# One queue for every load and store, row copies for the gathers, and 64-column value products in a windowed-attention kernel with token routing

## The chip, the cores and the metric

The kernel runs on one core of a Trainium2 chip. Its time is the device time of one execution in microseconds (us), the median over runs. All other times come from one profiled execution of the kernel before, counted from the start of its span. TensorE is called PE, VectorE DVE, ScalarE ACT, GpSimd POOL and SyncE SP, as in the profile.

## What is computed

Attention with a sliding window of 128 positions and 4 sink tokens, over 4 batches, 8 heads, 768 positions and 64 columns a head; then, in each batch, the 128 tokens with the highest gate score go through a two-layer network and are added back.

```python
scores = scale * np.matmul(q, k.transpose(0, 1, 3, 2))
keep = is_sink | in_window
scores = np.where(keep, scores, -1000000000.0)
a = softmax(scores)                       # cut: max, exp, sum
attn = np.matmul(a, v)                    # [4, 8, 768, 64] -> x [4, 768, 512]
...
scores = np.einsum('bsd,d->bs', x, w_gate)
for b in range(B):
    top_idx = np.argpartition(-scores[b], capacity)[:capacity]    # capacity = 128
    xe = x[b, top_idx]
    ye = np.maximum(xe @ w1, 0.0) @ w2                            # 512 -> 1024 -> 512
    g = 1.0 / (1.0 + np.exp(-scores[b, top_idx]))
    out[b, top_idx] = x[b, top_idx] + g[:, None] * ye
```

## The kernel before

**Steps.** The main loop has 30 steps. Batch 0 takes 12 half steps (steps 0 to 5 for four of its heads, then 6 to 11 for the other four, six blocks j of 128 positions each); batches 1, 2 and 3 take six full steps each (12 to 17, 18 to 23, 24 to 29; all eight heads). The order of all work is written out by hand: functions are hung on a step with `before` (ahead of the step), `middle`, `at` (after its normalisation) and `late`, and each engine executes its instructions in exactly that order.

**One step.** `scores` for step i+2 (PE, into PSUM, then an exponential on ACT, L251); `values` of step i (PE): sink products (L272) and products of the probabilities with the values, 65 columns wide, since a column of ones gives the softmax sum; `norm` (DVE): reciprocal (L300) and two multiplications (L303) into the row tile x; `gate_score` (DVE, L307): the gate's dot product. `values` has one pair of PSUM banks, X, so the products of step i+1 start when `norm` of step i has read it. `store` (L512) sends x of step i-1 to the output from SP's queue.

**Value products.** The stationary operand is a piece of the probabilities, float32, 128 or 64 rows by 64 query columns; each product becomes two PE instructions. Most are 64 columns wide (L262), and two or four of them stand in different parts of the array. For heads 4 to 7 the middle block is one product with 128 columns (L285), except at j = 1, where the key of the sink products makes two 64-column products of it (L281 to L284).

**Loads.** A "head pair" (k and q of two heads, 384 KB each) is loaded by `load_pair` (L126), cast to bf16 by `cast_pair` (mostly POOL, L141), transposed on PE (L172), and copied out of PSUM by DVE (L177) or ACT (L179). Batch 0's pairs come through SP's and ACT's queues at the start; all others through POOL's queue, batch 1's at step 2, batch b+1's right behind the casts of batch b (L585 to L589). Values are loaded in chunks of 128 positions (`load_v`, L143) through SP's queue: batch 1's seven chunks all ahead of step 0, batch 2's one a step from step 8, batch 3's from step 14 (L521 to L524). The weights w1 and w2 are loaded by POOL at step 22, and the first waits for chunk 3 of batch 3 (L528 to L534).

**Ranks.** For batches 0 and 1 the gate scores go to memory (`bounce_out`, L310, into srow) and back as one row broadcast to all partitions (`bounce_in`, L313, into sbc); both DMAs are issued by ACT, in the middle of steps 12 and 13 (18 and 19 for batch 1). `rank_c` (DVE, L317) counts the larger scores, `select` (L348) makes a selection matrix, `chosen` (L353) turns it into row numbers idx. Batches 2 and 3 rank on the chip (`spread`, `compare`, `overtake`).

**Gather and scatter.** `gather` (L380, POOL, indirect DMA) reads the chosen rows from the output tensor for batches 0 to 2, where the row number counts from the tensor's start, and from the row copy xrow for batch 3, which `store` also writes. The network is `ffn_cast` (POOL, L390), `ffn_in`, `ffn_1`, `ffn_2`, `ffn_out`; the last scatters the rows into the output with another indirect DMA (L417). Regions of the output and the row copies are tracked: a gather over rows [0, 2x768) of the output and a scatter into rows [0, 768) are ordered by a wait.

**Semaphores.** The program gives the DMAs of SP and ACT eight completion semaphores in rotation, in the order in which the program is written, whichever of the two issues them; a DMA is issued once the one that held its semaphore before has landed.

Of the kernel before, what the change touches and what calls it, by code (L numbers as in the profile page):

```python
# [8 lines left out]
FP32 = mybir.dt.float32  # L9
# [6 lines left out]
B = 4  # L16
# [17 lines left out]
def kernel(  # L34
# [46 lines left out]
    rankl = [one([128, NB], FP32, "rankl"), x0[:, NB - 2, 16:16 + NB]]  # L81
# [27 lines left out]
    xrow = tc.dram_tile([S, DM], FP32, name="xrow")  # L109
    idl = x0[:, NB - 2, 0:1].bitcast(U32)  # L110
# [15 lines left out]
    def load_pair(b, hp, eng=pool):  # L126
        hs = slice(2 * hp, 2 * hp + 2)
        for t, src in enumerate((k, q)):
            eng.dma_start(out=raw[2 * hp + t][:, :, :, :].rearrange("p h c d -> p h (c d)"),
                          in_=src[b, hs, :, :].rearrange("h (p c) d -> p h (c d)", c=NB))  # L130
# [122 lines left out]
    def values(b, j, heads, bank, which):  # L253
# [26 lines left out]
        for hh in heads:  # L280
            if j == 1:  # L281
                mm(1, 0, hh, FULL, j, 1, j)
                mm(1, 1, hh, FULL, j, 2, j)
                continue  # L284
            pe.matmul(out=ps[:, bank + 1, hh * SK:hh * SK + SK], lhsT=p[j][:, HP + hh, 64:192],  # L285
                      rhs=s.v[1][:, hh, j, 0:SK], start=(1, 0) not in seen, stop=False, skip_group_check=True)
            seen.update(((1, 0), (1, 1)))
# [22 lines left out]
    def bounce_out(b):  # L310
        act.dma_start(out=srow[b, :].rearrange("(p c) -> p c", c=NB), in_=st[b].scol[:, :])

    def bounce_in(b):  # L313
        act.dma_start(out=sbc[:, :], in_=srow[b, :].partition_broadcast(128))
# [38 lines left out]
    def chosen(b, bank, e=E):  # L353
# [6 lines left out]
        if b == B - 1:  # L360
            chl = x0[:, NB - 2, 8:9]
            dve.tensor_scalar_add(out=chl[:, :], in0=ch[:, 1:2], scalar1=-float((B - 1) * S))
        dve.tensor_scalar(out=idx[b][:, :], in0=ch[:, 0:1], scalar1=128.0, scalar2=ch[:, 1:2],
                          op0=ALU.mult, op1=ALU.add)
        if b == B - 1:
            dve.tensor_scalar(out=idl[:, :], in0=ch[:, 0:1], scalar1=128.0, scalar2=chl[:, 0:1],
                              op0=ALU.mult, op1=ALU.add)
# [12 lines left out]
    def gather(b):  # L380
        if b == B - 1:
            src, ix, n = xrow, idl, S
        else:
            src, ix, n = flat, idx[b], (b + 1) * S
        pool.indirect_dma_start(out=xe[b % 3][:, :], out_offset=None, in_=src[0:n, :],
                                in_offset=bass.IndirectOffsetOnAxis(ap=ix[:, 0:1], axis=0),
                                bounds_check=n - 1, oob_is_err=False)
# [33 lines left out]
    with tc.manual_schedule():  # L421
# [3 lines left out]
        load_pair(0, 0, sp)  # L425
        load_pair(0, 2, act)
        load_v_first(0)
        load_pair(0, 1, sp)
        load_pair(0, 3, sp)
# [78 lines left out]
        def store(i):  # L508
# [4 lines left out]
            if b == B - 1:  # L513
                sp.dma_start(out=xrow[j * 128:(j + 1) * 128, :], in_=xt[(b, j)])
# [6 lines left out]
        for c in range(NB + 1):  # L521
            before(0, lambda c=c: load_values(1, c))
            before(8 + c, lambda c=c: load_values(2, c))
            before(14 + c, lambda c=c: load_values(3, c))  # L524
# [3 lines left out]
        def load_weights():  # L528
            for n in range(2):
                i = pool.dma_start(out=w1_sb[:, 2 * n:2 * n + 2, :], in_=w1r[:, 2 * n:2 * n + 2, :])  # L530
                if n == 0:
                    after(i, arrived[(B - 1, 3)])
# [20 lines left out]
        for b, i, js in ((0, 12, (14, 15, 16, 16, 17, 18)), (1, 18, (20, 21, 22, 23, 24, 25))):  # L553
# [24 lines left out]
        for hp in range(HP):  # L578
            before(2, lambda hp=hp: load_pair(1, hp))
# [5 lines left out]
        for b, i0 in ((1, 6), (2, 12), (3, 18)):  # L585
            for hp in range(HP):
                before(i0 + hp - 2, lambda b=b, hp=hp: cast_pair(b, hp))
                if b < B - 1:
                    before(i0 + hp - 2, lambda b=b, hp=hp: load_pair(b + 1, hp))  # L589
# [32 lines left out]
        for i, (b, j, g) in enumerate(steps):  # L622
# [26 lines left out]
            if i == 5:  # L649
                pool.iota(iota_i[:, :], pattern=[[1, 128]], base=0, channel_multiplier=0)  # L650
                pool.iota(tk_i[:, 0:B, :], pattern=[[NB, B], [1, NB]], base=0, channel_multiplier=0)
# [71 lines left out]
```

The softmax here doesn't subtract the row's maximum and nothing guards it: scores larger than these inputs give would overflow.

## Time and profile before

| | |
|---|---|
| time, median of 3 runs (lowest to highest) | 162.63 us (162.05 to 163.7) |
| span of the profiled execution | 161.5 us |
| PE busy | 133.3 us (82%), 2595 instructions |
| PE weight loads busy | 103.5 us (64%) |
| DVE busy | 91.9 us (57%) |
| ACT busy | 78.5 us (49%) |
| POOL busy | 75.6 us (47%) |
| moved by DMA | 32.41 MB, 201 GB/s over the span |
| value products with 128 columns, L285 | 160 instructions, 24.2 us, 291 ns each |
| value products with 64 columns, L262 | 1120 instructions, 38.6 us, 232 ns each |
| head pairs from POOL's queue | 24 DMAs of 384 KB, 7.4 and 7.6 us from issue to landing |

Busy time is the union of the time in which an engine executes; matmuls overlap, so the mean length of one is far above the distance from one to the next, and only the timeline shows the latter. Instructions that issue DMAs don't count as busy. An engine's idle time is put down to what ended it; where a wait has several causes, to the one that came last. A busy share over the whole span hides that stretches have different bounds, so stretches are looked at one by one.

### The profile page before, as it was taken

The numbers are of one execution on the slowest core, as the hardware profiler recorded it, in microseconds if no ns is written. First come the engines' busy times: TensorE is split into PE (matmuls) and PEld (weight loads), VectorE is DVE, ScalarE is ACT, GpSimd is POOL, SyncE is SP. The second block draws the span as 40 slices with busy tenths as digits, with TensorE's granted clock in tenths as the row PEclk, the third lists the DMA queues.
The fourth block names the chain that finished last, engine by engine and source line by source line (L and its number), as shares of the span: only waits on it lengthen the run. The fifth ranks groups of instructions, "written<-read, shape, count | busy, mean of one in ns | idle before, by whom it ended". The sixth has DMA issues, their size and how long they took to land. (4 is left out here: it accounts for less than half of the span.)

```text
span 161.5 us, 6069 instructions
## 1 busy us (share of the span) xinstructions
PE 133.3 (82%) x2595; PEld 103.5 (64%) x2599; DVE 91.9 (57%) x283; ACT 78.5 (49%) x106; POOL 75.6 (47%) x123
## 2 busy tenths in 40 slices
PE   6697989998999029979999997999899599986820
PEld 2255767786788016777788886788776389765500
DVE  6831351568447300664989687779957817376310
ACT  3269266577770043965657578566355102131300
POOL 8637999996997500219106148301202544040520
PEclk9999999999999965999999999999999956999985
DMA  4999899999799998942474343999616333040311
GB/s 111 364 232 343 195 234 381 394 371 365 211 361 339 366 359 238 245 137 86 130 203 140 109 134 80 202 203 235 224 50 199 127 133 127 7 189 10 96 46 55
DMA packets 37658, 32.41 MB, mean 201 GB/s; under 512 B 26992, under 2 KB 30448, under 8 KB 37632
## 3 DMA queue, kind: packets, MB, share of 16 engines
q1 hardware_dynamic: 31456, 16.78, 36.6%
q0 software_dynamic: 5056, 13.67, 27.4%
q10 hardware_dynamic: 1120, 1.58, 3.5%
q8 instruction: 20, 0.33, 0.8%
q14 instruction: 6, 0.05, 0.1%
HBM read 25.20 MB, written 8.92 MB: 211 GB/s over the span
## 5 line engine op out<-in xcount | busy, mean ns | idle before, releaser
L251 ACT ACTIVATE pt<-ps 128x1024 f32<-128x1024 f32 x48 | 47.2, 1034 | 5.8 <-PE ps L229 4.6
L262 PE MATMUL ps<-vbuf,pt 64*64 64x65 f32 (+1 forms) x1120 | 38.6, 232 | 0.7 <-DVE x L303 0.7
L262 PEld LDWEIGHTS ps<-vbuf,pt 64*64 64x64 f32 (+1 forms) x1120 | 30.5, 140 | 11.8 <-issue 8.3
L300 DVE RECIPROCAL rz<-ps 128x8 f32<-128x8 f32 (+1 forms) x30 | 5.9, 196 | 50.5 <-PE ps L262 50.5
L186 POOL COPY ksk<-KT 64x4 bf16<-64x4 bf16 x32 | 9.1, 284 | 33.2 <-ACT KT L179 15.1
L285 PE MATMUL ps<-vbuf,pt 128*128 128x65 f32 x160 | 24.2, 291 | 0.0
L141 POOL CAST kq<-raw 128x768 bf16<-128x768 f32 x28 | 23.1, 852 | 1.7 <-DMA raw<-in_k_dram 0.8
L179 ACT COPY QT<-ps 128x768 bf16<-128x768 bf16 x16 | 12.9, 803 | 19.0 <-DMA out_dram<-x 11.1
L285 PEld LDWEIGHTS ps<-vbuf,pt 128*128 128x128 f32 x160 | 20.7, 199 | 1.8
L172 PE MATMUL ps<-ident_b,kq 128*128 128x128 bf16 x192 | 14.4, 225 | 8.5 <-ACT QT L179 7.1
L213 PE MATMUL ps<-QT,KT 64*64 64x192 bf16 (+2 forms) x384 | 17.4, 248 | 4.6 <-ACT QT L179 2.6
L303 DVE TENSOR_TENSOR x<-ps,rz 128x256 f32<-128x256 f32 (+1 forms) x60 | 19.5, 366 | 1.2
L307 DVE CUSTOM_DVE_ANT_0 junk<-x,wgb 128x512 f32<-128x512 f32 x24 | 19.0, 794 | 0.4
L172 PEld LDWEIGHTS <-kq 128*128 128x128 bf16 x192 | 11.6, 100 | 10.8 <-issue 7.2
L213 PEld LDWEIGHTS <-KT 64*64 64x64 bf16 x384 | 10.5, 107 | 9.8 <-issue 5.9
L272 PE MATMUL ps<-vsk,psk 64*64 64x260 f32 (+1 forms) x180 | 15.6, 358 | 0.9 <-DVE x L303 0.9
L229 PE MATMUL ps<-mask,ident_b 64*64 64x256 bf16 (+1 forms) x208 | 15.3, 264 | 0.0
L317 DVE TENSOR_SCALAR_CACHE_REDUCE junk<-sbc,scol 128x768 bf16<-128x768 f32 x12 | 12.2, 1012 | 0.4
L646 POOL CAST x<-x 128x512 bf16<-128x512 f32 x6 | 4.2, 706 | 15.5 <-DVE x L303 8.8
L323 ACT COPY sbl<-ps 128x128 f32<-128x128 f32 x12 | 3.1, 260 | 15.7 <-PE ps L321 15.7
L417 POOL DMA_INDIRECT out_dram<-y,idx x4 | 4.1, 1023 | 13.8 <-DVE y L415 10.1
L177 DVE COPY KT<-ps 128x768 bf16<-128x768 bf16 x10 | 9.5, 951 | 1.5 <-PE ps L172 1.5
(94 smaller groups left out, 170.9 us busy)
## 6 DMA issues: line engine op xcount, KB each, us to landing
out_dram<-x SPq DMA_DIRECT2D x24, 256.0 KB, 3.7
raw<-in_k_dram POOLq DMA_DIRECT2D x12, 384.0 KB, 7.4
raw<-in_q_dram POOLq DMA_DIRECT2D x12, 384.0 KB, 7.6
vbuf<-in_v_dram SPq DMA_DIRECT2D x33, 128.0 KB, 5.3
w_sb<-in_moe_w_dram POOLq DMA_DIRECT2D x4, 512.0 KB, 9.8
xrow<-x SPq DMA_DIRECT2D x6, 256.0 KB, 3.9
raw<-in_k_dram SPq DMA_DIRECT2D x3, 384.0 KB, 4.0
raw<-in_q_dram SPq DMA_DIRECT2D x3, 384.0 KB, 5.0
```

What stands on the lines that cost most here:

```text
L141: (eng or pool).tensor_copy(out=o, in_=i)
L172: pe.transpose(out=trp[:, c, :], in_=src[:, c, :, :].rearrange("p h d -> p (h d)"), identity=ident_b[:, :])
L179: act.copy(out=o, in_=i)
L213: pe.matmul(out=sc[64 * m:64 * m + 64, e, a, o:o + n], lhsT=s.KT[r, hp, k0:k0 + 64], rhs=s.QT[r, hp, k0:k0 + n], start=a == 0, stop=False, ...
L229: pe.matmul(out=o, lhsT=ident_b[r, r], rhs=w[r].unsqueeze(1).to_broadcast((64, a.stop - a.start, 2, 64)), start=False, stop=True, skip_gro ...
L251: act.activation(out=po[:, gi, :, :, :], in_=sc[:, :, :, :], func=ACT.Exp, scale=0.125)
L262: pe.matmul(out=ps[64 * c:64 * c + 64, bank + be, hh * SK:hh * SK + SK], lhsT=p[i][rows, h, 64 * slot:64 * slot + 64], rhs=s.v[be][rows, h ...
L272: pe.matmul(out=ps[64 * c:64 * c + 64, bank + be, a * SK:z * SK], lhsT=s.psk[which][r, c, 64 * (j - 1):64 * j], rhs=vsk[r, b, be, a:z, :], ...
L285: pe.matmul(out=ps[:, bank + 1, hh * SK:hh * SK + SK], lhsT=p[j][:, HP + hh, 64:192], rhs=s.v[1][:, hh, j, 0:SK], start=(1, 0) not in seen ...
L303: dve.tensor_tensor(out=xo[:, e, :, :], in0=xg[:, e, :, 0:D], in1=rz[:, e, 0:n, :].to_broadcast((128, n, D)), op=ALU.mult)
L307: dve.tensor_tensor_reduce(out=junk[:, :], in0=x, in1=wgb[:, :], scale=1.0, scalar=0.0, op0=ALU.mult, op1=ALU.add, accum_out=st[b].scol[:, ...
L317: dve.tensor_scalar(out=junk[:, :].bitcast(BF16)[:, 0:S], in0=sbc[:, :], scalar1=st[b].scol[:, c:c + 1], scalar2=0.0, op0=ALU.is_gt, op1=A ...
```

## The change

It has four parts.

1. **One queue.** `load_pair` uses SP by default (batch 0's pair 2 stays on ACT); so do `bounce_out` and `bounce_in`. After the start, ACT issues no DMA, and POOL only the weights, the gathers and the scatters.
2. **Order of need.** Pairs of batch 1 are loaded one a step at steps 0 to 3, batch 2's at 6, 8, 9 and 11, batch 3's at 13 to 16. Values of batch 1 come one chunk a step from step 4, batch 2's from step 12, batch 3's from step 16. The weights wait for chunk 5 of batch 3. Batch 0's ranks move by a step here and there (step 14 no longer has one).
3. **Row copies.** Batches 1, 2 and 3 each get a row copy; `store` writes every row tile of these twice, and `gather` reads from the copy with row numbers counted from the batch's start. Only batch 0's gather reads the output. `chosen` makes two row numbers, for the gather (idl) and for the scatter (idx).
4. **64-column products.** `values` uses two 64-column products for the middle block of heads 4 to 7 at every j.

It is meant to keep transfers from colliding, to free ACT and POOL from issuing them, to take the order between gathers and scatters away, and to use the form of product that keeps parts of the array working side by side.

```diff
-    def load_pair(b, hp, eng=pool):
+    def load_pair(b, hp, eng=sp):
...
         for hh in heads:
-            if j == 1:
-                mm(1, 0, hh, FULL, j, 1, j)
-                mm(1, 1, hh, FULL, j, 2, j)
-                continue
-            pe.matmul(out=ps[:, bank + 1, hh * SK:hh * SK + SK], lhsT=p[j][:, HP + hh, 64:192],
-                      rhs=s.v[1][:, hh, j, 0:SK], start=(1, 0) not in seen, stop=False, skip_group_check=True)
-            seen.update(((1, 0), (1, 1)))
+            mm(1, 0, hh, FULL, j, 1, j)
+            mm(1, 1, hh, FULL, j, 2, j)
...
     def bounce_out(b):
-        act.dma_start(out=srow[b, :].rearrange("(p c) -> p c", c=NB), in_=st[b].scol[:, :])
+        sp.dma_start(out=srow[b, :].rearrange("(p c) -> p c", c=NB), in_=st[b].scol[:, :])
     def bounce_in(b):
-        act.dma_start(out=sbc[:, :], in_=srow[b, :].partition_broadcast(128))
+        sp.dma_start(out=sbc[:, :], in_=srow[b, :].partition_broadcast(128))
...
-        dve.tensor_scalar(out=idx[b][:, :], in0=ch[:, 0:1], scalar1=128.0, scalar2=ch[:, 1:2],
+        dve.tensor_scalar(out=(idl[b] if b else idx[0])[:, :], in0=ch[:, 0:1], scalar1=128.0, scalar2=ch[:, 1:2],
                           op0=ALU.mult, op1=ALU.add)
-        if b == B - 1:
-            dve.tensor_scalar(out=idl[:, :], in0=ch[:, 0:1], scalar1=128.0, scalar2=chl[:, 0:1],
+        if b:
+            chl = x0[:, NB - 2, 32:33]
+            dve.tensor_scalar_add(out=chl[:, :], in0=ch[:, 1:2], scalar1=float(b * S))
+            dve.tensor_scalar(out=idx[b][:, :], in0=ch[:, 0:1], scalar1=128.0, scalar2=chl[:, 0:1],
                               op0=ALU.mult, op1=ALU.add)
...
     def gather(b):
-        if b == B - 1:
-            src, ix, n = xrow, idl, S
-        else:
-            src, ix, n = flat, idx[b], (b + 1) * S
-        pool.indirect_dma_start(out=xe[b % 3][:, :], out_offset=None, in_=src[0:n, :],
+        src, ix = (xrow[b], idl[b]) if b else (flat, idx[0])
+        pool.indirect_dma_start(out=xe[b % 3][:, :], out_offset=None, in_=src[0:S, :],
...
             sp.dma_start(out=out[b, j * 128:(j + 1) * 128, :], in_=xt[(b, j)])
-            if b == B - 1:
-                sp.dma_start(out=xrow[j * 128:(j + 1) * 128, :], in_=xt[(b, j)])
+            if b:
+                sp.dma_start(out=xrow[b][j * 128:(j + 1) * 128, :], in_=xt[(b, j)])
...
-            before(0, lambda c=c: load_values(1, c))
-            before(8 + c, lambda c=c: load_values(2, c))
-            before(14 + c, lambda c=c: load_values(3, c))
+            before(4 + c, lambda c=c: load_values(1, c))
+            before(12 + c, lambda c=c: load_values(2, c))
+            before(16 + c, lambda c=c: load_values(3, c))
...
-                    after(i, arrived[(B - 1, 3)])
+                    after(i, arrived[(B - 1, 5)])
...
-        for b, i, js in ((0, 12, (14, 15, 16, 16, 17, 18)), (1, 18, (20, 21, 22, 23, 24, 25))):
+        for b, i, js in ((0, 12, (15, 15, 16, 17, 17, 18)), (1, 18, (20, 21, 22, 23, 24, 25))):
...
-        for hp in range(HP):
-            before(2, lambda hp=hp: load_pair(1, hp))
+        for b, at_ in ((1, (0, 1, 2, 3)), (2, (6, 8, 9, 11)), (3, (13, 14, 15, 16))):
+            for hp, i in enumerate(at_):
+                before(i, lambda b=b, hp=hp: load_pair(b, hp))
...
                 before(i0 + hp - 2, lambda b=b, hp=hp: cast_pair(b, hp))
-                if b < B - 1:
-                    before(i0 + hp - 2, lambda b=b, hp=hp: load_pair(b + 1, hp))
```

## The prediction

> **What bounds the kernel now.** I read the map of the span in 40 slices first, to see where TensorE (PE) is busy and where its clock is low.
>
> ```profile
> PE   6697989998999029979999997999899599986820
> DVE  6831351568447300664989687779957817376310
> ACT  3269266577770043965657578566355102131300
> PEclk9999999999999965999999999999999956999985
> DMA  4999899999799998942474343999616333040311
> ```
>
> PE is 80 to 100% busy in nearly all slices between 8 and 145 us, so its instruction stream sets the pace. Three exceptions: a hole in slices 13 and 14, counted from 0 (52 to 60 us), a halved clock behind it, and a second halved clock in slices 32 and 33 (129 to 137 us). The DMA row is at 9 until 64 us and low afterwards.
>
> The timeline around the hole says who made it:
>
> ```profile
> 51.12 2.21 SPq L512 DMA_DIRECT2D out_dram<-x  x1
> ...
> 58.38 0.35 ACTq L311 DMA_DIRECT2D srow<-scol  x1
> 58.77 0.80 ACT L179 COPY QT<-ps 128x768 bf16<-128x768 bf16 x1 [11.14 <-DMA out_dram<-x]
> ...
> 59.62 0.69 PE L172 MATMUL ps<-ident_b,kq 128*128 128x128 bf16 x5 [7.12 <-ACT QT L179]
> ```
>
> ScalarE (ACT) does nothing for 11.14 us: the small DMA of L311 stands in its instruction stream, and the program gives hardware DMAs eight completion semaphores in rotation, so L311 must wait for the DMA eight before it, a store in SyncE's (SP's) backlogged queue. PE waits behind ACT for 7.12 us. The table by stretch gives the size:
>
> ```profile
> 52.50:59.60 7.10, 0.00 (x0) 0.00 (x0) 1.34 (x4) 0.83 (x2) 2.06 (x3) 0.86 1.09 368
> 59.60:66.00 6.40, 6.09 (x96) 4.62 (x96) 0.00 (x0) 3.83 (x5) 0.36 (x2) 0.62 0.92 241
> ...
> 126.00:128.50 2.50, 0.59 (x7) 0.31 (x3) 2.40 (x9) 0.36 (x2) 2.25 (x3) 1.00 0.26 100
> 128.50:137.00 8.50, 8.47 (x104) 7.38 (x104) 4.20 (x15) 1.45 (x3) 3.29 (x4) 0.60 0.43 153
> ```
>
> Columns: length, busy time of PE, weight loads, VectorE (DVE), ACT, POOL, then granted clock, DMA share, GB/s. No matmul in the first stretch, clock 0.62 and 0.60 in the stretches behind both gaps.
>
> Last, the timeline of two whole steps, j=1 of batch 2 and j=2 of batch 2:
>
> ```profile
> 84.88 1.78 PE L262 MATMUL ps<-vbuf,pt 128*64 128x65 f32 x64
> ...
> 86.58 0.49 PE L321 MATMUL ps<-ident_f,scol 128*128 128x128 f32 x2
> ...
> 88.78 0.69 PE L262 MATMUL ps<-vbuf,pt 128*64 128x65 f32 x16
> ...
> 89.40 1.11 PE L285 MATMUL ps<-vbuf,pt 128*128 128x65 f32 x8
> ...
> 90.43 0.69 PE L262 MATMUL ps<-vbuf,pt 64*64 64x65 f32 x32
> ...
> 91.06 0.30 PE L356 MATMUL ps<-tok,E 128*128 128x4 bf16 x6
> ```
>
> This is the measurement of the new form inside the old kernel. Step j=1 already uses 64-column products only: 64 matmuls from 84.88 to the next work at 86.58, 1.70 us. Step j=2 computes the same with 128-column products: 16 + 8 + 32 matmuls from 88.78 to 91.06, 2.28 us. Its eight 128-column ones take 89.40 to 90.43, 129 ns each; the 64-column ones before them 39 ns each (0.62 over 16).
>
> **What the Trainium skill says.** "TensorEngine Tiling (Array Packing)", Key Properties: a change of tiling mode drains the array, and different tiles run in parallel. The trace agrees on the second: 39 ns against 129 ns with twice as many instructions; a drain is not shown apart. "TensorE: Matmul & The Clock Gate", What's actually happening: the clock halves after an idle window of about 3.4 us and returns after a busy one. The 7.1 us hole agrees. The second dip follows a stretch in which PE worked 0.59 of 2.5 us, shorter than that window, so here a nearly idle window was enough. "DMA: Bandwidth & Descriptors", Issuing engines are not separate DMA queues: moving transfers between engines saves issue time only, all share 16 engines. The trace agrees in that the share stands near 1.0 up to 64 us, whichever queues feed it.
>
> **The change, part by part.**
>
> *64-column products.* Per full step (batches 1 to 3, not j=1): 2.28 - 1.70 = 0.58 us of PE. Per half step of batch 0: 1.36 us with 128 columns (17.86 to 19.22) against 0.85 and 1.01 for the two j=1 half steps, so 0.35 to 0.51, taken as 0.43. Batch 0 has 10 such half steps, each on the path since the next products wait for DVE's normalisation of these: 4.3 us. For full steps I check DVE, which needs its own time per step. Between normalisations it is busy without idle in steps 18, 23 and 24 (3.55 of 3.69 us in 106.28:109.97, 4.25 of 4.39 in 109.97:114.36): those give nothing, step 18 the 0.3 us that DVE waited. Left are steps 12, 14 to 17, 20 to 22 and 26 to 29: 12 x 0.58 + 0.3 = 7.3 us. Between both bounds (all 15: 8.7; half: 4) I take 7.3.
>
> *ACT's small DMAs go to SP.* The hole goes: 7.1 us. The slow stretch 59.6 to 66.0 (transposes, scores, products) takes 6.4 us and at full clock about 4.5 (0.4 for the rest of the transposes, 1.2 for scores, 2.9 for sink and other products, as at 72.8 to 75.7): 1.9 us. Sum 9.0. ACT's later bounce (81 to 87 us) costs PE nothing now.
>
> *Loads just in time, pairs from POOL to SP.* POOL loses 24 issues of 0.72 us, 17.4 us; its casts are ahead of need (PE waits for POOL 0.7 us in all), so worth nothing by itself. The question is whether SP keeps up. In order of SP's queue I add up the bytes (pair 0.79 MB, a chunk of values 0.26, a store 0.26): start 5.0 MB, all of batch 1's pairs 8.1, step 6 9.6, step 12 14.6, step 13 16.6, step 17 22.4. Rates of the trace: 315 GB/s between 12.9 and 46.1 us, 382 in its best quarter. At 350 these are there at 16, 25, 29, 44, 49 and 66 us. PE would want batch 1's last pair at about 34 us, batch 2's first at 43, step 13's rank row at 55, step 17's loads only 3 or more steps later than 63. So hidden, but with little slack for the two rank rows (sbc, 4.2 us to landing, behind srow, 4.1): DVE's rank instructions would stand in front of a normalisation. Bounds 0 and 8 us; I take 1 us for each row, 2.0.
>
> *Row copies.* 12 more stores (3.1 MB, 0.4 us of SP each); from 80 us on the DMA row is mostly at 3 or 4, so the later ones hide. Gather 1 no longer conflicts with scatter 0, which POOL held from 123.3 to 126.2 us (idle 3.4 before L417), nor gather 2 with its landing. The cast for FFN 1 thus comes earlier than 127.84, and PE's wait for it (0.7, weight loads 0.9) goes: 0.8 us. PE's other wait there, 1.2 us for the copy of the chosen tokens (L321 on DVE ch), stays, as its order on DVE does. So I leave the second clock dip in the forecast. DVE gains two small operations in two selections, 0.15 + 0.21 us each, beside PE work.
>
> *Tail.* From the last products (139.9) to the end the chain of selection and FFN is unchanged: 0.
>
> Sum: 162.6 - 4.3 - 7.3 - 9.0 - 0.8 + 2.0 = 143.2 us.
>
> **Rivals.**
> 1. *The second clock dip goes too, and SP keeps up.* The gap at 126 us shrinks from 2.4 to about 1.9 us. Work of 128.5 to 137 at full clock: products 2.3 instead of 3.9, FFN 1.95 instead of 2.9, sink products and spread 0.5 less, so 3.0 us, and 2.0 of waits fewer: 138.2. For it: the gap was a near miss by the skill's window; against: the 1.2 us wait stays.
> 2. *DMA takes over.* Everything is in one queue in order, each DMA waits for the eighth before it, and steps 13 to 16 each want 1.5 MB in 3.4 us, 440 GB/s, over any rate in the trace. At 305 GB/s (36.5 to 46.1) the 23 MB up to step 18 end at 77 us, where PE would be at about 64; with 5 us of order slack in the stores' four buffers, 8 us more: 151. For it: the full DMA row up to 64 us. Against: what is late by then is needed latest.
> 3. *Slower.* SP stands at a bounce (srow landing before sbc) while loads queue behind it; DVE stands at ranks, PE goes cold each time. To lose, new waits must exceed 21 us: three holes like the old one, 7.1 + 1.9 each, give 143.2 - 2.0 + 27 = 168. For it: the old hole had just this form, one DMA behind another's landing. Against: it now stands in SP, where nothing computes.
>
> **How the numbers follow.** Forecast 0.52, rival 1 0.25, rival 2 0.17, rival 3 0.06. The range runs from 137 (rival 1 with all 15 steps gained) to 152 (rival 2) and leaves out rival 3 and some edges. Faster by over 1%: 0.93, within 1%: 0.02, slower: 0.05.
>
> **What would show it.** Right: no L285-like 128*128 product group, the products of a full step in 1.7 us; no ACT wait on a DMA; PE over 80% busy at 45 to 60 us; clock 1.0 there. Wrong: DVE idle before a rank (L312 in the new file) on sbc, normalisation or casts waiting on a store or load, PE idle behind them; or steps that keep their length with DVE full, which would mean that the products were not the bound.

## The result, and the profile after

The changed kernel takes 152.33 us (median of 4 runs, 149.12 to 154.33), the kernel before 162.34 us beside it. The ratio, 0.922 with a 95% interval of 0.909 to 0.936, leaves out executions that are over 1.5% above the fastest of their kernel, as the ratios below do, so here it is that of 149.12 and 150.53 us; the medians of all would give 0.938. The forecast of 143.2 us was too low by 9 us against the median, which lies 0.3 us above the upper end of its range, 137 to 152, and by 6.6 us against the mean of those two, which lie inside it. Executions of one kernel differ here by 3 us and more, so below a total is given as a median with its lowest and highest, and what a part is worth is read from the traces. Each trace is one execution; where it is a long one of its kernel, the text says so.

The profiled execution of the changed kernel took 150.53 us, its span is 148.8 us. Its map in 40 slices (3.7 us each):

```profile
PE   6687989998989987669799920998989969977940
DVE  6851172569438464098988306778996696688520
ACT  3169467598887875365746780055827232323310
PEclk9999999999999999999999997589999999999995
DMA  3999969987999999999999799899995346332031
```

The hole at 52 to 60 us and the low clock behind it are gone, and so is the low clock near the end (slices 32 and 33). A new hole stands in slices 23 and 24 (86 to 93 us): PE at 2 and 0, DVE at 0 in the first of them, then a clock of 0.5 to 0.8. The DMA row is at 6 to 9 until slice 29 (112 us), where it used to fall at 64 us.

The table by stretch (length, busy time of PE, weight loads, DVE, ACT, POOL, then clock, DMA share, GB/s), the first three where the old hole and its surroundings were:

```profile
42.80:49.80 7.00, 7.00 (x192) 5.93 (x188) 4.78 (x14) 5.06 (x7) 2.49 (x3) 1.00 1.08 355
52.50:59.60 7.10, 5.55 (x160) 4.32 (x157) 3.88 (x10) 4.82 (x6) 3.76 (x9) 1.00 0.98 275
59.60:66.00 6.40, 3.85 (x104) 2.82 (x100) 2.92 (x7) 3.43 (x5) 2.18 (x4) 1.00 1.11 355
82.30:92.90 10.60, 4.35 (x126) 3.46 (x117) 2.90 (x11) 5.83 (x8) 2.36 (x5) 0.90 0.95 273
92.90:98.00 5.10, 5.07 (x76) 3.91 (x78) 3.34 (x12) 0.02 (x1) 3.62 (x5) 0.54 0.88 212
123.00:129.90 6.90, 6.90 (x181) 5.69 (x179) 4.27 (x15) 2.30 (x6) 3.17 (x4) 1.00 0.53 186
```

PE works where it stood before, but only 5.55 of 7.1 us and 3.85 of 6.4 us. The fourth and fifth line are the new hole and its cold clock.

The timeline says what the new hole waits for. Step 17 is the last block of batch 1; its gate score is read at 70.46 us:

```profile
70.46 0.08 DVE L302 DVE_READ_ACCUMULATOR2_ANT scol<- 128x1 f32 x1
...
80.22 0.41 SPq L306 DMA_DIRECT2D srow<-scol  x1
...
82.92 1.78 PE L262 MATMUL ps<-vbuf,pt 128*64 128x65 f32 x64
83.97 0.32 SPq L309 DMA_DIRECT2D sbc<-srow  x1
...
90.70 1.01 DVE L312 TENSOR_SCALAR_CACHE_REDUCE junk<-sbc,scol 128x768 bf16<-128x768 f32 x1 [7.63 <-DMA sbc<-srow]
...
92.93 1.46 PE L272 MATMUL ps<-vsk,psk 64*64 64x260 f32 x8 [5.47 <-DVE x L298]
```

SP issues the small DMA of the row 9.8 us after the score is there. DVE then stands 7.63 us at the first rank instruction (L312), behind it the normalisation of step 21 (L298), behind that PE. SP hardly idled in these 9.8 us: fourteen issues of loads and stores lie between, 0.4 to 1.2 us each, 8.5 us together; why one takes three times as long as another is open. None of them waited for a landing: wherever it is recorded (thirteen of the fourteen), the DMA eight places earlier had landed before SP was free. In the table of waits:

```profile
DVE junk L312 <- DMA sbc<-srow: 11.9, 2, 7.6
...
PE ps L272 <- DVE x L298: 8.6, 5, 5.5
```

(Columns: total us, number, longest.) The products of a full step now take 1.78 us for 64 matmuls (the line at 82.92), as in step j=1 before.

For what follows I cut each trace at the start of DVE's reciprocal of certain steps. "End" is the end of the span. The forecast's column puts its terms into the same stretches: 0.43 us for each half step and 0.58 for each full step it counted (a step's products lie ahead of its own reciprocal), 9.0 for the hole, 1.0 for each row, 0.8 for the cast.

| stretch | before | after | difference | forecast |
|---|---|---|---|---|
| start to step 0 | 14.46 | 14.01 | -0.4 | -0.4 |
| steps 0 to 12 | 34.04 | 30.62 | -3.4 | -4.5 |
| steps 12 to 20 | 42.70 | 35.57 | -7.1 | -11.2 |
| steps 20 to 22 | 10.61 | 17.27 | +6.7 | -0.2 |
| steps 22 to 27 | 24.13 | 23.54 | -0.6 | -1.2 |
| steps 27 to 29 | 14.07 | 8.99 | -5.1 | -2.0 |
| step 29 to end | 21.5 | 18.8 | -2.7 | 0 |
| sum | 161.5 | 148.8 | -12.7 | -19.4 |

Two stretches lost 10.9 us against the forecast, steps 12 to 20 and 20 to 22; the last two gained 5.8 more than it had.

### The profile page after: what moved, and what is told of

Read it like the earlier page. It is cut to its first block, busy times and chain, and to the rows that moved or that the text cites. A ratio compares the mean times of both kernels' runs of the same rounds, so it can differ in the third digit from the quotient of the medians.

```text
span 148.8 us, 6421 instructions
## 1 busy us (share of the span) xinstructions
PE 120.2 (81%) x2755; PEld 91.6 (62%) x2759; DVE 91.5 (62%) x287; ACT 78.5 (53%) x106; POOL 58.8 (40%) x99
## 2 busy tenths in 40 slices
DMA packets 43227, 35.57 MB, mean 239 GB/s; under 512 B 27184, under 2 KB 36400, under 8 KB 43200
## 5 line engine op out<-in xcount | busy, mean ns | idle before, releaser
L262 PE MATMUL ps<-vbuf,pt 64*64 64x65 f32 (+1 forms) x1440 | 47.6, 230 | 3.6 <-issue 2.9
L262 PEld LDWEIGHTS ps<-vbuf,pt 64*64 64x64 f32 (+1 forms) x1440 | 40.7, 139 | 15.3 <-issue 11.8
L272 PE MATMUL ps<-vsk,psk 64*64 64x260 f32 (+1 forms) x180 | 16.5, 359 | 8.6 <-DVE x L298 8.6
L298 DVE TENSOR_TENSOR x<-ps,rz 128x256 f32<-128x256 f32 (+1 forms) x60 | 19.5, 366 | 1.6 <-DMA xrow<-x 0.4
L312 DVE TENSOR_SCALAR_CACHE_REDUCE junk<-sbc,scol 128x768 bf16<-128x768 f32 x12 | 12.2, 1013 | 12.3 <-DMA sbc<-srow 11.9
L302 DVE CUSTOM_DVE_ANT_0 junk<-x,wgb 128x512 f32<-128x512 f32 x24 | 18.0, 750 | 0.4
L172 PE MATMUL ps<-ident_b,kq 128*128 128x128 bf16 x192 | 13.6, 220 | 1.6 <-ACT kq L139 1.5
L272 PEld LDWEIGHTS ps<-vsk,psk 64*64 64x64 f32 x180 | 7.7, 135 | 10.3 <-DVE x L298 8.9
L172 PEld LDWEIGHTS <-kq 128*128 128x128 bf16 x192 | 11.1, 98 | 3.7 <-ACT kq L139 1.7
L394 PE MATMUL ps<-xeT,w_sb 128*128 128x128 bf16 x128 | 8.0, 219 | 0.7 <-ACT xeT L387 0.7
L394 PEld LDWEIGHTS <-w_sb 128*128 128x128 bf16 x128 | 7.4, 98 | 1.1 <-DVE y L406 0.9
```

The costliest lines, as they stand in the source:

```text
L172: pe.transpose(out=trp[:, c, :], in_=src[:, c, :, :].rearrange("p h d -> p (h d)"), identity=ident_b[:, :])
L262: pe.matmul(out=ps[64 * c:64 * c + 64, bank + be, hh * SK:hh * SK + SK], lhsT=p[i][rows, h, 64 * slot:64 * slot + 64], rhs=s.v[be][rows, h ...
L272: pe.matmul(out=ps[64 * c:64 * c + 64, bank + be, a * SK:z * SK], lhsT=s.psk[which][r, c, 64 * (j - 1):64 * j], rhs=vsk[r, b, be, a:z, :], ...
L298: dve.tensor_tensor(out=xo[:, e, :, :], in0=xg[:, e, :, 0:D], in1=rz[:, e, 0:n, :].to_broadcast((128, n, D)), op=ALU.mult)
L302: dve.tensor_tensor_reduce(out=junk[:, :], in0=x, in1=wgb[:, :], scale=1.0, scalar=0.0, op0=ALU.mult, op1=ALU.add, accum_out=st[b].scol[:, ...
L312: dve.tensor_scalar(out=junk[:, :].bitcast(BF16)[:, 0:S], in0=sbc[:, :], scalar1=st[b].scol[:, c:c + 1], scalar2=0.0, op0=ALU.is_gt, op1=A ...
```

## The experiments

The theory to be tested: the products and the hole are worth what the forecast said, and what is missing was lost to the rows that come late, and to transfers and issues that PE now runs into. Rivals: the products were never the bound; or the DMA engines are full, so that nothing can come earlier. Lines quoted carry the numbers of their own kernel, which are off by a few where lines were added.

### One part at a time, in the kernel before

**64-column products alone.**

```diff
-            if j == 1:
-                mm(1, 0, hh, FULL, j, 1, j)
-                mm(1, 1, hh, FULL, j, 2, j)
-                continue
-            pe.matmul(... lhsT=p[j][:, HP + hh, 64:192], ...)
+            mm(1, 0, hh, FULL, j, 1, j)
+            mm(1, 1, hh, FULL, j, 2, j)
```

> The kernel before with part 4 alone: the middle block of heads 4 to 7 as two 64-column products at every j. Theory A (PE's stream of products sets the pace of the steps, as the prediction had it): 4.3 us from batch 0 and 7.3 us from the full steps go, the hole at 52 to 60 us stays, so about 151 us (149 to 153). Rival B (the freed PE time is taken by other waits: DVE's normalisations and ranks, ACT's exponentials, the loads): half of it or less is seen, 156.5 us or more. Two numbers to read in the trace: products of step j=2 of batch 2 in about 1.7 us instead of 2.28 in both cases, step lengths from 14 to 18 and 18 to 22 shorter by about 2 us each with A, by less than 1 us with B.

Measured: 157.06 us (155.37 to 159.68), before 162.64 beside it: -5.6 us, half of the forecast, so B by its total. Of the two step lengths named, 18 to 22 fell by 1.7 us (16.99 instead of 18.70), near A's 2; 14 to 18 grew by 4.2 us, with the clock at half from 64 to 70 us, while 12 to 14 fell by 8.2: the hole did not stay as it was, so that stretch doesn't measure the products. Steps 0 to 12 grew too, from 34.04 to 35.69 us. The timeline of PE has this in them:

```profile
26.28 0.27 PE L229 MATMUL ps<-mask,ident_b 64*64 64x256 bf16 x1
28.59 0.30 PE L229 MATMUL ps<-mask,ident_b 64*64 64x256 bf16 x3 [2.04 <-issue]
```

PE stands for 2.04 us between two matmuls of one kind, on nothing that the trace knows ("issue"), and the clock is at 0.69 in 25.8 to 36.9 us. The kernel before has no such wait of PE anywhere. Steps 27 to 29, where nothing of this kind happens, did get shorter: 12.41 instead of 14.07.

**The two small DMAs from POOL instead of ACT.**

```diff
-        act.dma_start(out=srow[b, :]...)      # bounce_out
+        pool.dma_start(out=srow[b, :]...)
-        act.dma_start(out=sbc[:, :]...)       # bounce_in
+        pool.dma_start(out=sbc[:, :]...)
```

> The kernel before with the two small DMAs of the ranks (L311 and L314) issued by POOL instead of ACT; all else as before. Theory A (the hole comes from ACT standing at the issue of L311, and only from that): ACT has no wait on a DMA, PE is over 80% busy from 52 to 60 us, the clock stays at 1.0 there, and the time falls by the hole and its cold clock, 9 us, to about 153.5 us (152 to 155.5). Rival B (the backlog of transfers reaches PE by another way as soon as ACT is free, through the casts that stand behind the row in POOL's stream, or through the ranks): at least half of the 9 us comes back elsewhere, 158 us or more, with PE idle behind POOL or behind a rank.

Measured: 159.06 us (155.32 to 163.3), by its median B, with a spread of 8 us. In the trace (156.88 us) steps 12 to 14 took 8.7 us instead of 17.6, so the hole is gone (A): PE is busy for 7.36 of the 8 us from 52 to 60 at a clock of 1.0, and ACT waits for no DMA but the loads of the start. Steps 12 to 20 took 35.97 instead of 42.70, 6.7 us less: DVE waited 4.5 us at a rank for the row sbc, and some of the gain went there. The other stretches are as before to 0.1 us, apart from a start 1.6 us later (the last section says why) and an end 1.2 us shorter.

**Both together.**

> The kernel before with two edits: part 4 (64-column products) and the two small DMAs of the ranks issued by POOL. Loads, their order and the row copies as before. The two edits alone gave -5.6 and -3.6 us (medians). Theory A (the two gains add, and the new order of loads and the row copies of the change bring nothing on balance): 151 to 154 us, as fast as the changed kernel with the same move of the small DMAs to within 4 us. Rival B (without the order of need the faster PE runs into late loads between steps 12 and 20): 156 us or more, with PE idle behind casts that wait for a pair. In the trace: reciprocal of step 12 to that of step 20 in about 31 us with A (36.4 us in the changed kernel with the small DMAs on POOL), 35 us or more with B.

Measured: 154.07 us (151.35 to 158.03): the sum of the two gains (-9.2 us) is there, as A said. Its trace is that of the longest execution (158.03 us): steps 12 to 20 took 35.02 us in it, which is B's number, and PE's waits on "issue" came to 8.4 us. This kernel has neither the order of need nor the additional row copies, and its median is within 2 us of the changed one's, but 4.4 us above that of the changed one with the same move of the small DMAs (149.71 us, next section), a little more than the 4 that A allowed.

### Parts of the change undone

**128-column products again**, all else as in the changed kernel (the first diff, reversed).

> The changed kernel with part 4 undone: the middle block of heads 4 to 7 as one 128-column product, except at j=1. Theory A (products are on the path also in the changed kernel, apart from the two places where it waits for a row sbc): 4.3 us for batch 0 and about 5 us for the full steps come back, so about 161 us (158.5 to 163). Rival B (the changed kernel is bound by transfers, so longer products only fill waits): less than 3 us come back, 155 us or less, and the DVE wait on sbc shrinks by as much as the products grow.

Measured: 157.58 us (156.66 to 157.73), so part 4 is worth 5.3 us in the changed kernel by the medians and 7.0 us between the two traces (spans of 155.8 and 148.8 us), between the two theories. Step 0 to step 20 took 67.06 us with 128 columns and 66.19 us with 64: up to there the faster form brought 0.9 us, where the forecast had 7.7. Of the rest 4.2 us lie in steps 27 to 29, where the low clock of the kernel before is back. PE waits on "issue" nowhere in this run.

**The two small DMAs from POOL, in the changed kernel** (as in the diff above, with `sp` instead of `act`).

> The changed kernel with the two small DMAs of the ranks issued by POOL instead of SP; all loads and stores stay in SP's queue. Theory A (the rows are late because they stand in SP's queue, behind the waits and the bytes of loads and stores issued ahead of them): DVE's wait on sbc falls from 11.9 us to under 4 us, the low clock at 92 to 98 us goes, and the time falls by 6 to 9 us, to 141.5 to 146 us. Rival B (all 16 DMA engines are full, so that the small transfers are as late from any queue, or POOL stands at them and its casts come late): DVE or PE wait as long as now and the time stays within 2 us of the changed kernel.

Measured: 149.71 us (147.8 to 151.37). A was right on the rows and wrong on the time. From the timeline of its longest execution:

```profile
73.19 0.08 DVE L302 DVE_READ_ACCUMULATOR2_ANT scol<- 128x1 f32 x1
...
73.56 0.54 POOL L306 DMA_DIRECT2D srow<-scol  x1 [0.85 <-DVE scol L302]
...
79.95 0.54 POOL L309 DMA_DIRECT2D sbc<-srow  x1
...
115.92 1.14 PE L401 MATMUL ps<-w_sb,hT 128*128 128x512 bf16 x4 [3.08 <-DMA w_sb<-in_moe_w_dram]
```

Batch 1's row leaves 0.4 us after its score instead of 9.8, and its second DMA 6.8 us after it instead of 13.5; DVE waits 1.5 us for the rows instead of 11.9, and steps 20 to 22 take 10.26 us instead of 17.27. The DMA itself was not faster: the row that comes back took 6.3 us from issue to landing (batch 0's, the one recorded), 6.6 us in the changed kernel (batch 1's). So the lateness was made in SP's stream of issues, not in flight. Batch 0's row stands in POOL's stream behind casts that wait for pairs, and left 5.7 us after its score (45.12 and 50.78 us), against 8.3 from SP. But PE, 7 us earlier, then met the weights of the second layer, which were not there, stood 3.08 us and ran at a low clock behind it: steps 22 to 27 took 28.15 us instead of 23.54.

**No row copies for batches 1 and 2.**

```diff
-        src, ix = (xrow[b], idl[b]) if b else (flat, idx[0])
+        src, ix, n = (xrow, idl, S) if b == B - 1 else (flat, idx[b], (b + 1) * S)
...
-            if b:
+            if b == B - 1:
                 sp.dma_start(out=xrow[...], in_=xt[(b, j)])
```

> The changed kernel with part 3 undone: batches 1 and 2 are gathered from the output, only batch 3 has a row copy; 3.1 MB fewer bytes. Theory A (bytes bind between 45 and 108 us, and the copies are a good part of them): DVE's wait on sbc falls from 11.9 to under 6 us, steps 20 to 24 lose their low clock, the low clock near the end (gather waiting for scatter and stores) returns and costs 4 us: 148 to 151 us. Rival B (the rows are late because of their place in SP's queue, not because of the bytes): the wait on sbc stays above 9 us and the end becomes 4 us longer: 154 to 157 us.

Measured: 152.77 us (150.01 to 156.76). The waits went as A had them; the median is a little above its band, and the fastest execution, 150.01 us, whose trace this is, lies in it:

```profile
DVE junk L312 <- DMA sbc<-srow: 3.0, 2, 2.3
...
PE ps L390 <- POOL xeb L385: 1.7, 1, 1.7
```

With 12 issues and 3.1 MB less, DVE waits 3.0 us for the rows instead of 11.9, and steps 20 to 22 take 10.23 us. What the copies were for came back: PE waits 1.7 us for the cast of the gathered rows, the clock falls to 0.57 in 116 to 124 us, and steps 27 to 29 take 13.30 us instead of 8.99. The copies thus gain 4.3 us at the end and cost as much or more in the middle, as long as the rows leave from SP; from POOL, the run before, steps 20 to 22 take 10.26 us with all copies in place.

**Ranks at later steps.**

```diff
-(0, 12, (15, 15, 16, 17, 17, 18)), (1, 18, (20, 21, 22, 23, 24, 25))
+(0, 12, (16, 16, 17, 17, 18, 18)), (1, 18, (22, 22, 23, 23, 24, 25))
```

> The changed kernel with the rank instructions at later steps: batch 0 at 16, 16, 17, 17, 18, 18 instead of 15, 15, 16, 17, 17, 18, batch 1 at 22, 22, 23, 23, 24, 25 instead of 20 to 25. The small DMAs stay in SP's queue at their place. Theory A (a late row costs only because DVE stands at it in front of a normalisation): DVE's wait on sbc falls from 11.9 to under 3 us, the low clock at 92 to 98 us goes, 143 to 146 us. Rival B (the core is bound by the transfers up to 110 us, so that a step that comes earlier finds something else late): another wait takes its place, for casts, for weights or at the fuller DVE of steps 22 to 25, 148 us or more.

Measured: 151.76 us (150.32 to 152.97), so B by the time, though A's wait did vanish: no wait on sbc is left, and steps 20 to 22 take 9.48 us. Steps 22 to 27 take 28.83. The table in stretches of 2 us shows the loss:

```profile
99.00:101.00 2.00, 1.15 (x29) 0.73 (x28) 1.96 (x6) 1.34 (x3) 0.44 (x1) 1.00 0.97 210
101.00:103.00 2.00, 1.49 (x6) 0.68 (x8) 1.94 (x5) 1.36 (x2) 0.61 (x1) 0.55 1.08 251
```

DVE, now with more ranks in these steps, is full (1.96 of 2 us), PE waits here and there behind it, and after a stretch in which it worked 1.15 of 2 us its clock is at half for 10 us; within these it also waits 1.27 us for the weights of the first layer.

**The old loads, with copies and 64 columns.** Pairs from POOL's queue and early, values at steps 0, 8 and 14 on, the weights behind chunk 3, as in the kernel before; row copies and products as in the changed one; small DMAs on POOL.

> The changed kernel with parts 1 and 2 undone for the loads: pairs again from POOL's queue and early, values at steps 0, 8 and 14 on, weights behind chunk 3; 64-column products and all three row copies stay; the two small DMAs of the ranks are on POOL. Theory A (loads just in time are what holds the changed kernel between steps 12 and 20, since the DMA share stays at 1.0 up to 108 us and casts wait for pairs): steps 12 to 20 take about 31 us instead of 36.4, no wait of PE for weights near 115 us, the low clock at 129 to 137 us of the kernel before stays away, 143 to 147 us. Rival B (the loads in order of need help, and the row copies' 3.1 MB are what holds it): 149 us or more.

Measured: 152.22 us (147.01 to 153.51), B by its median, but the fastest execution is at the edge of A's band, so the total doesn't decide. In the trace (153.27 us) there is no wait on sbc, none for weights and no low clock at the end (A), but steps 0 to 12 took 34.42 us and 12 to 20 36.87 us, with 8.8 us of PE's waits on "issue". So in this execution loads just in time are not what holds PE there, or not alone.

### How much do transfers and issues take from the products?

These two kernels leave work out: k and q of batches 2 and 3 are not loaded, the casts take what batch 1 left in the buffers.

```diff
-for b, at_ in ((1, (0, 1, 2, 3)), (2, (6, 8, 9, 11)), (3, (13, 14, 15, 16))):
+for b, at_ in ((1, (0, 1, 2, 3)),):
```

> The changed kernel without the loads of k and q of batches 2 and 3 (16 DMAs of 384 KB, 6.3 MB of 35.6): these batches compute on what batch 1 left in the buffers, so their part of the output is not the reference's. All instructions of PE, DVE, ACT and POOL stay. Theory A (from step 12 to step 20 transfers set the pace: every kernel with the loads in order of need reached step 20 some 66 to 67.4 us after step 0, with either form of product): step 0 to step 20 falls to 58 to 61 us, the row sbc comes in time (DVE's wait on it under 3 us), PE's own waits for nothing that is shown (3.5 us in the changed kernel) fall below 1 us, 139 to 144 us in all. Rival B (the chain of PE, DVE and ACT sets the pace there and the full DMA row is only a sign): step 0 to step 20 stays above 64 us, 147 us or more.

> The same kernel, without the loads of k and q of batches 2 and 3, but with the 128-column products of the kernel before (its output differs from the reference's in the same part). Against the run with 64-column products it measures part 4 where fewer transfers are under way. Theory A (part 4 is worth the 11.6 us of the prediction when nothing else binds, and the 5 us seen so far are what transfers let through): 9 to 12 us longer than the run with 64 columns. Rival B (the prediction's price of a step was too high by itself, DVE and ACT take half of it in any case): 4 to 6 us longer.

Measured: 141.05 us (139.43 to 141.33) with 64 columns, ratio to before 0.858 (0.851 to 0.865); 149.34 us (147.29 to 151.97) with 128, ratio 0.911 (0.904 to 0.919). The first is in A's band, though step 0 to step 20 took 61.83 us, just above A's 61, and PE's waits on "issue" stayed at 2.8 us where A wanted less than 1. The second is 8.3 us longer by the medians and 7.7 us between steps 0 and 29 of the traces, between its two theories. Steps 12 to 20, the changed kernel first, then the one without these loads:

```profile
44.60:80.20 35.60, 30.31 (x822) 24.03 (x823) 24.45 (x63) 22.70 (x27) 15.71 (x26) 1.00 1.06 322
```

```profile
46.60:77.50 30.90, 28.85 (x822) 23.32 (x823) 23.62 (x64) 22.52 (x27) 13.17 (x22) 1.00 0.82 230
```

The same 822 matmuls take 4.7 us less, most of it idle time of PE (5.3 against 2.1 us). Its row of batch 1 is issued 0.9 us after the score (67.98 and 68.92 us in its timeline), against 9.8. With 128 columns, step 0 to step 20 takes 67.07 us without the loads and 67.06 with them: the slow products leave room for every transfer and every issue, the fast ones do not.

| stretch | 64 columns | 128 columns | worth | forecast |
|---|---|---|---|---|
| steps 0 to 12 | 31.00 | 34.04 | 3.0 | 4.5 |
| steps 12 to 20 | 30.83 | 33.03 | 2.2 | 3.2 |
| steps 20 to 22 | 9.66 | 10.90 | 1.2 | 1.2 |
| steps 22 to 27 | 24.22 | 24.28 | 0.1 | 1.2 |
| steps 27 to 29 | 8.98 | 10.12 | 1.1 | 1.2 |
| sum | 104.7 | 112.4 | 7.7 | 11.1 |

The 2.8 us on "issue", 2.5 of them in steps 22 to 27, occur with 64 columns only. Step by step the price is clearer than in the sums. Of the eleven full steps after step 12 that the forecast counted at 0.58 us, nine are shorter with 64 columns by 0.53 to 0.70 us, six of them by 0.57; the other two, 15 and 26, gain nothing or grow, and each has one of these waits in it (0.32 and 1.10 us).

### A version that beats both

Four edits to the changed kernel: small DMAs on POOL, a row copy for batches 1 and 3 only, the weights behind chunk 3, and three dummy products between the first pair's transposes of k and of q.

```diff
-        sp.dma_start(out=srow[b, :]...)
+        pool.dma_start(out=srow[b, :]...)
-        sp.dma_start(out=sbc[:, :]...)
+        pool.dma_start(out=sbc[:, :]...)
-            if b:
+            if b in (1, 3):
                 sp.dma_start(out=xrow[b][...], in_=xt[(b, j)])
-        src, ix = (xrow[b], idl[b]) if b else (flat, idx[0])
+        src, ix, n = (xrow[b], idl[b], S) if b in (1, 3) else (flat, idx[b], (b + 1) * S)
-                    after(i, arrived[(B - 1, 5)])
+                    after(i, arrived[(B - 1, 3)])
+            if b == 0 and hp == 0 and t == 1:
+                for i in range(3):
+                    pe.matmul(out=ps[:, i, :], lhsT=zb[:, 0:128], rhs=zb[:, :], ...)
```

> The changed kernel with four edits: the two small DMAs of the ranks on POOL; no row copy for batch 2 (1.6 MB less; its gather reads the output); the weights wait for chunk 3 of batch 3 instead of chunk 5; three more dummy products on PE between the first pair's transposes of k and of q, so that its clock isn't lowered at 8 to 11 us where the start is a little late (1.5 us in the runs with a late start). Theory A (each wait has its own cause, seen above): no low clock at 8 to 12 us, DVE's wait on sbc under 2 us, no wait of PE for w2, no low clock at 120 to 130 us: 144.5 to 147.5 us. Rival B (any gain before step 20 only brings PE earlier to late transfers): 149 us or more, with PE idle behind casts, weights or in itself.

Measured: 146.86 us (145.1 to 147.3), ratio to before 0.891 (0.883 to 0.898), which does not overlap the changed kernel's 0.909 to 0.936. Each wait named is gone: no wait on sbc, none for weights, no low clock at the start or near the end, steps 20 to 22 in 10.38 and 27 to 29 in 8.99 us; batch 1's copy alone is enough for the latter. What is left is mostly in steps 12 to 20, 36.82 us. The timeline of PE has these waits, the first two in that stretch, among others:

```profile
52.93 1.71 PE L266 MATMUL ps<-vbuf,pt 128*64 128x65 f32 x61 [0.79 <-issue]
59.40 0.74 PE L266 MATMUL ps<-vbuf,pt 128*64 128x65 f32 x17 [2.17 <-issue]
...
98.99 0.28 PE L217 MATMUL ps<-QT,KT 64*64 64x192 bf16 x4 [1.05 <-issue]
105.88 0.69 PE L266 MATMUL ps<-vbuf,pt 64*64 64x65 f32 x31 [1.30 <-issue]
```

The one of 2.17 us is followed by 3.4 us at half the clock, from 60.9 us on.

**The slow product where PE stands most.** The same kernel with 128 columns in steps 12 and 14 to 18.

```diff
-            mm(1, 0, hh, FULL, j, 1, j)
-            mm(1, 1, hh, FULL, j, 2, j)
+            if not (b == 1 and j != 1 or (b, j) == (2, 0)):
+                mm(1, 0, hh, FULL, j, 1, j)
+                mm(1, 1, hh, FULL, j, 2, j)
+                continue
+            pe.matmul(... lhsT=p[j][:, HP + hh, 64:192], ...)
```

> The kernel of the run with four edits (146.86 us), with the 128-column form of product again in steps 12 and 14 to 18 alone, the stretch in which the DMA row stands at 1.0 and PE most often stands for no shown cause; 64 columns in batch 0 and from step 19 on. These products take longer by themselves (steps 12 to 20 took 33.03 us with them and 30.83 without where fewer bytes were loaded) but are 48 pairs of load and product fewer. Theory A (with 64 columns PE runs through its instructions there faster than they come to it past the transfers): PE's waits for nothing that is shown fall from 8.1 us to about 5, steps 12 to 20 from 36.8 to 33 to 34.5 us, the whole to 143.5 to 145.5 us. Rival B (the late pairs hold PE there, whatever the form): steps 12 to 20 stay at 36 us or more, 146.5 us or more.

Measured: 147.54 us (145.28 to 149.01): no difference in the time beyond the spread, so the total doesn't decide (median on B's side, the fastest in A's band). In the trace (148.06 us) PE's waits on "issue" did fall, from 8.1 to 3.5 us, and steps 12 to 20 from 36.82 to 35.23 us, between the theories, although these products are slower. In their place POOL's casts waited 13.5 us for pairs (5.7 before), and DVE 2.9 us for a row. Both limits lie there close together, and taking one away shows the other.

## Why the prediction was right or wrong

The mechanism, term by term: the hole and the price of a full step were right, the rank rows were mis-sized, PE's waits on "issue" had no term, and the second clock dip, which the forecast kept, went. That the miss is not larger is in part luck: the last two stretches gained 5.8 us more than forecast, 2.7 of them unexplained.

**The hole, -9.0: right in its place.** Steps 12 to 14 went from 17.6 to 7.6 us in the changed kernel, and to 8.7 us with nothing but the small DMAs taken from ACT. In that run 6.7 us of the 8.9 were left at step 20, since DVE then waited 4.5 us for a row.

**The rank rows, +2.0: the step that failed.** The forecast had taken "1 us for each row, 2.0" between bounds of 0 and 8. DVE waited 11.9 us for them, 4.3 for batch 0's and 7.6 for batch 1's, and steps 20 to 22 alone became 6.7 us longer, with the cold clock behind the hole. The reason it gave, "with little slack for the two rank rows", was right, but the slack was worked out from bytes over a rate and from the time in flight (4.2 and 4.1 us). SP's own time was left out: batch 1's row stood in SP's stream behind fourteen issues of 8.5 us together, and left 9.8 us after its score. "0.4 us of SP each", said of the row copies and called hidden, was part of this: without twelve of them the wait fell to 3.0 us. The forecast leaned on "DMA: Bandwidth & Descriptors", Issuing engines are not separate DMA queues, by which issuing from more engines saves only the time to initiate. The runs agree with that and show that this time can be the bound: from POOL a row took as long to land (6.3 against 6.6 us), and batch 1's left 9.4 us sooner. Against rival 3 the forecast had said that the wait "now stands in SP, where nothing computes": true, but what stood in SP's stream was what DVE waited for.

**64-column products, -11.6: the price of a full step right, that of a half step too high, and a good part given back.** In the run with the fewest transfers they are worth 7.7 us. In batch 0 a half step gains some 0.3 us and not 0.43. Nine of eleven full steps gain what was forecast; the other two contain waits on "issue", which only this form has, 2.8 us in all, and the forecast had no term for them. In the changed kernel 5.3 us (medians) or 7.0 us (traces) of the 11.6 are left, 4.2 of the latter in steps 27 to 29, where the clock has a part: up to step 20 PE runs into SP's backlog and into those waits.

**Rival 2, "DMA takes over", 151 us at 0.17**, came nearest to the time, and to the place (steps 13 to 18). Its mechanism was half right: it added up bytes, and less traffic did give 4.7 us in steps 12 to 20. How much of that is bytes, and how much issues, these runs don't separate, since each load left out is both.

**The copies, -0.8: too small, and rival 1 was right there.** The forecast left the second clock dip in; with the copies it never occurs in a kernel with 64 columns and the end takes 5.1 us less. In the changed kernel with 128 columns it does occur (13.2 us), in the same without the loads of two batches it does not (10.1 us): a near miss, as rival 1 had it (the last section has the two windows of the clock, 2.20 and 2.19 us of work).

**Tail, 0: wrong by 2.7 us, and open.** It took 18.7 to 20.1 us in the kernels with the new order of loads, and 20.3 to 21.5 in those with the old one, whatever the products. No run was aimed at it.

**Of the signs named beforehand**, those for right came (no wait of ACT, products in 1.7 to 1.8 us, clock 1.0 at 45 to 60 us), and so did the first for wrong: DVE idle before L312 on sbc, PE behind it. PE at 45 to 60 us was 90% busy (13.45 of 15 us), where over 80% was asked; in the place of the old hole alone, 52.5 to 59.6 us, it was 78%.

## What to carry to other kernels

When loads and stores move into one queue, add up its issues as well as its bytes, and follow the one small transfer that someone waits for: it comes after all that was written ahead of it. Give it a queue with nothing in front of it: here batch 1's row then left after 0.4 instead of 9.8 us, batch 0's, with casts in front of it, after 5.7 instead of 8.3. In a kernel with several limits close together a removed wait is not a gain until the next one is known: of the runs that took a wait away from the changed kernel and did all its work, only those with all four edits were clearly faster than it.

## What the hardware showed that was not expected

**PE stands at fixed places in its instruction stream.** In every kernel with 64-column products PE has waits on "issue" of 0.2 to 2.4 us, at different places in different runs, but all from one ladder. The matmuls recorded before each wait (as many weight loads) are, for the changed kernel, 1115, 1243, 2008, 2135 and 2263; for the one with small DMAs on POOL 987, 1243, 1371 and 1753; for the one with four edits 350, 476, 987, 1115, 1371, 1498, 1753, 2008 and 2135; for 64 columns alone 350, 2008 and 2134. The steps are multiples of 128 (a few records are missing), so 256 instructions with the loads. The page of the changed kernel has a queue that only carries instructions:

```profile
q8 instruction: 21, 0.34, 0.9%
```

That is 16 KB a packet, and "Perfetto Trace Analysis", The 4-stage abstract model, gives an instruction as 64 bytes, which makes 256. The number of packets says that they are PE's: 21 where PE has 5514 recorded instructions (21.5 times 256), 20 in the kernel before, where it has 5194 (20.3 times). So a wait stands where a new block begins.

The records of the single packets in the traces show the cause. All 55 waits of the fourteen traces end 1.2 to 1.7 us after one of these packets has ended, and in the nine kernels with 64 columns everywhere PE never passed a place of the ladder sooner than 1.2 us after its packet, with a wait or without. The packets that PE waited for were not slow themselves (0.9 to 1.3 us); they started late, 2.1 to 5.6 us after PE had passed the place before. In the changed kernel after 114.5 us, where the DMA row is low, they started 0.2 to 1.1 us after it, and no kernel has such a wait after 115 us. That they start late because other transfers stand ahead of them is inferred: the waits occur only where the DMA row is near full, and are fewer with fewer bytes (2.8 against 3.6 us). With 128 columns, whose products take 129 instead of 39 ns each, they sum to 0.65 us in one kernel and to nothing in three.

**A nearly idle stretch is enough to halve the clock, and where its window lies decides near misses.** Over 6 to 8 us PE worked 0.46 of 2 us in the changed kernel and kept its clock. In the kernel without copies, from the tables of 2 us at the start, it did not:

```profile
4.00:6.00 2.00, 1.20 (x6) 0.27 (x4) 1.43 (x10) 0.00 (x0) 2.00 (x3) 1.00 1.07 399
6.00:8.00 2.00, 0.49 (x6) 0.32 (x6) 1.83 (x7) 0.78 (x2) 1.03 (x4) 0.98 1.16 339
8.00:10.00 2.00, 1.89 (x9) 1.07 (x10) 0.49 (x1) 1.59 (x3) 0.36 (x2) 0.50 1.28 227
```

PE had 1.20 instead of 1.93 us of work in the stretch before, and step 0 came 1.9 us later (15.90 against 14.01). Its first pair came 0.3 us later (first cast on ACT at 7.22 instead of 6.89 us), but that is not the cause: the run with both edits had its first cast at 6.88 us and lost its clock, the changed kernel with 128 columns at 7.28 us and kept it. "TensorE: Matmul & The Clock Gate", What's actually happening, has a free-running window of 3.4 us, so that the point of the change varies from run to run. The records of the clock agree: in all fourteen traces the time from one change to the next is a whole multiple of 3.41 us, and the changes fall at different times in each. But the window need not be idle. I added up PE's busy time in each window at full clock. All 34 windows with less than 1.6 of 3.41 us were followed by half the clock, none of the 470 with more than 2.3; of the 35 between, 7 were. In the eight traces with a late start the window there began at 4.1 to 5.6 us and had 1.2 to 1.6 us of work; in the other six it began at 5.5 to 6.7 us and had 1.8 us or more. The two with three dummy products in the gap are among the six, with 2.5 and 2.6 us. The near miss at the end is one of the same kind: with 128 columns 2.20 us of work lost the clock, and 2.19 us, in the run with fewer loads, kept it.
